# A token-mixing kernel: first pair of each pass on raw operands, 64-row tiles at the pass change, eight operand blocks loaded early

## The chip, the cores and the metric

The kernel runs on one core of one Trainium2 chip. The metric is the device time of one execution in microseconds (us). A profiled execution has a span a little below its own time (2212.3 us for a run of 2214.05 us), and the profile of the kernel before happens to be of a run 3 us under the median. So differences between two profiles and differences between two medians do not agree to the microsecond.

Names of the engines: PE is TensorE, DVE is VectorE, ACT is ScalarE, POOL is GpSimd, SP is SyncE. SBUF is the on-chip memory that holds operands, PSUM the one into which products are written. The granted clock is TensorE's clock as the profile shows it, 1.00 being full. The DMA share is the mean busy share of the core's 16 DMA engines; it goes a little over 1 in these views, so it serves for comparison only. A name such as `L850` is line 850 of the kernel that the profile belongs to. Line numbers shift between kernels.

## The reference

The input `x` is (8, 5696, 128). A long convolution along the sequence comes first, then a mixing block. Cut to what matters:

```python
y = irfft(rfft(x, n=2*S, axis=1) * rfft(h, n=2*S, axis=0), n=2*S, axis=1)[:, :S]  # S = 5696
theta = y @ w_theta                          # 128 x 128
zr, zi = y * cos(theta), y * sin(theta)      # "the phases"
u = y + einsum('ts,bsd->btd', w_tok_r, zr) + einsum('ts,bsd->btd', w_tok_i, zi)   # "the mixing"
out = u + relu(u @ w_ch)                     # "the output steps"
```

The mixing is by far the largest part: two 5696 x 5696 matrices against 8 x 128 columns.

## The kernel before

What matters starts near 480 us with the second half of the phases and ends with the last output.

**The phases** transpose a tile of `y` on TensorE, copy it from PSUM (`y_ap`, VectorE), store the copy, compute cos and sin, and store `z` to device memory (`z_hbm`). While they run, the first operand blocks of the mixing are loaded:

```python
    def load_b(p, j, pool):                       # block j of pass p: two parts, 2 x 512 KB
        t_ = pool.tile([P, 7 * 1024], BF16, tag=f"b{j}", name=f"b{j}")
        for z in range(2):
            eng = nc.scalar if z and (p or j >= NE) else nc.sync      # NE = 4
            eng.dma_start(t_[:, z * 2048:(z + 1) * 2048], z_hbm[z, p, j].rearrange(...))
        ...
    def sum_b(bt):                                # operand sums of one block, 128x1024 each
        nc.vector.tensor_sub(bt[M3], b12, b22)
        nc.vector.tensor_sub(bt[M4], b21, b11)
        nc.vector.tensor_add(bt[M1], b11, b22)
        nc.vector.tensor_add(b12, b11, b12)       # in place: the raw operand is gone
        nc.vector.tensor_add(b21, b21, b22)       # in place
    ...
    for n, ti in enumerate(tile_order):
        phase_step(ti, 1)
        if n in (7, 15, 19):
            load_b(0, next(early), bpe)           # then the fourth after the loop
```

**The mixing** contracts in two passes, p = 0 and 1, over halves of the sequence. A pass has 11 operand blocks (`b0` to `b10`, 1 MB each) that stay in SBUF and are read by everything in the pass. It treats 22 *pairs* of 128-row tiles by a scheme of seven products in place of eight (as Strassen's), on sums of operands (`sum_b`) and sums of weights (`w_sum`): 7 x 22 = 154 products of 128x512 a pair. Weights come in by POOL's DMA queue into six buffers, are transposed by VectorE (`w_t`), and summed by VectorE. In pass 0 the results go to device memory; in pass 1 they are fetched, added and turned into output ("output steps", woven between later products).

The last 64 rows make a *64-row tile* of 88 products in each pass, called `None` in the order:

```python
        pairs = (list(range(11)) + [None] + list(range(11, 22)), list(range(22)) + [None])
        ...
            if tt == 0:                           # before the products of the pass's first pair
                for j in range(nj):
                    sum_b(bts[j0 + s0 + j])
        ...
            for n, q in enumerate(ORDER):         # seven products
                for j in range(nj):
                    for r in range(2):
                        nc.tensor.matmul(ms[q], a[q][:, j, :, r], bts[jj][q][:, r, :], ...)
```

The blocks of pass 1 take the place of those of pass 0, so block j of pass 1 is loaded when the last reader of block j in pass 0 has finished. That stretch, from the end of pair 21 of pass 0 to the second pair of pass 1, is called the *pass change* below. Where a 64-row tile stands elsewhere, its 19.2 or 19.6 us are added to make kernels comparable.

Of the kernel before, what the change touches and what calls it, by code (L numbers as in the profile page):

```python
# [10 lines left out]
F32 = mybir.dt.float32  # L11
BF16 = mybir.dt.bfloat16
F16 = mybir.dt.float16
add = mybir.AluOpType.add
# [8 lines left out]
def kernel(  # L23
# [492 lines left out]
    ORDER = (M3, M4, M5, M2, M1, M7, M6)  # L516

    wp = ctx.enter_context(tc.tile_pool(name="wpool", bufs=6, side="right"))
    NE = 4
    bpe = ctx.enter_context(tc.tile_pool(name="bpool_e", bufs=1, side="right", reuse_waits="tile"))  # L520
    bts_of = {0: [], 1: []}

    def load_b(p, j, pool):

        t_ = pool.tile([P, 7 * 1024], BF16, tag=f"b{j}", name=f"b{j}")
        for z in range(2):
            eng = nc.scalar if z and (p or j >= NE) else nc.sync
            eng.dma_start(t_[:, z * 2048:(z + 1) * 2048],
                          z_hbm[z, p, j].rearrange("i (s r) n -> (i s) (r n)", r=2))
        bt = [t_[:, k * 2048:(k + 1) * 2048].rearrange("p (r q n) -> p r q n", r=2, q=2)[:, :, q, :]  # L530
              for k in range(2) for q in range(2)]
        bt += [t_[:, q * 1024:(q + 1) * 1024].rearrange("p (r n) -> p r n", r=2) for q in range(4, 7)]
        bts_of[p].append(bt)
# [8 lines left out]

    for step in steps0:
        step()
    early = iter(range(NE))
    for n, ti in enumerate(tile_order):
        phase_step(ti, 1)
        if n in (7, 15, 19):
            load_b(0, next(early), bpe)
    for j in early:  # L550
        load_b(0, j, bpe)
    pha.close()
    xa.close()
    psp.close()
# [3 lines left out]
    with tc.tile_pool(name="bpool", bufs=1, reuse_waits="tile") as bp, \  # L558
# [17 lines left out]
                            ap=[[S, 32], [32 * S, ng], [1, nj * 64]]))  # L576
            return wb

        def w_t(wb, j0, nj, ng=4):
            wt = tp.tile([P, TJ, P, 2], BF16, tag="wt")  # L580
            nc.vector.transpose(  # L581
                wt.rearrange("p j t r -> p (j t r)").bitcast(F32).rearrange(
                    "p (j g t) -> p g j t", j=TJ, g=4)[:, :ng, :nj],
                wb[:, :ng, j0 * 64:(j0 + nj) * 64].bitcast(F32).rearrange(
                    "p g (j s) -> p g j s", j=nj))
            return wt
# [125 lines left out]
                zl_of[p] = zl  # L712


        pairs = (list(range(11)) + [None] + list(range(11, 22)), list(range(22)) + [None])
        chunks = [(p, tt, c) for p in range(2) for tt in pairs[p] for c in range(len(CHUNKS))]
        stretches = []
        for k, (p, tt, c) in enumerate(chunks):
# [18 lines left out]
        def prepare(i, at_once=True):  # L737
            if i >= len(stretches):
                return None
            k, p, tt, j0, s0, nj = stretches[i]  # L740
            if s0 == 0:
                loads(k + 1)
            if tt is None:
                a1, a2 = (w_t(wb, s0, nj, ng=2) for wb in loaded[k])
                return a1, a2, w_sum(a1, a2, add, nj, m=64)
            w11, w22, w12, w21 = loaded[k]
            a = {}

            def step(n):

                if n == 0:
                    a[M3] = w_t(w11, s0, nj)
                elif n == 1:
                    a[M4] = w_t(w22, s0, nj)
                elif n == 2:
                    a["12"] = w_t(w12, s0, nj)
                    a[M5] = w_sum(a[M3], a["12"], add, nj)
                elif n == 3:
                    a["21"] = w_t(w21, s0, nj)
                    a[M2] = w_sum(a["21"], a[M4], add, nj)  # L760
                elif n == 4:
                    a[M1] = w_sum(a[M3], a[M4], add, nj)
                elif n == 5:
                    a[M7] = w_sum(a["12"], a[M4], ALU.subtract, nj)
                else:
                    a[M6] = w_sum(a["21"], a[M3], ALU.subtract, nj)
            if at_once:
                for n in range(7):
                    step(n)
                return a  # L770
            return a, step
# [3 lines left out]
        for i, (k, p, tt, j0, s0, nj) in enumerate(stretches):  # L775
            first_of_pair = j0 + s0 == 0
            end_of_pair = j0 + s0 + nj == NJ
            if first_of_pair and tt == 0:
                start_pass(p)
                if p == 0:  # L780
                    spread += [bg_phase(t, h) for t in list(range(22, 34)) + [44] + list(range(34, 44))
                               for h in range(2)]
                    spread += [bg_left(g) for g in range(0, NT, 4)]
                    spread[0][0]()
                    spread[1][0]()
                    nxt = prepare(0)
            bts, zl = bts_of[p], zl_of[p]
            if tt == 0:
                for j in range(nj):
                    sum_b(bts[j0 + s0 + j])  # L790

            woven = (tt is not None and end_of_pair and i + 1 < len(stretches)
                     and stretches[i + 1][2] is not None)
# [3 lines left out]
            if tt is None:  # L797


                if first_of_pair:  # L800
                    ps = [mps.tile([P, 512], F32, tag=f"m{q}", name=f"m{q}") for q in (M3, M4)]
                    cs = [addend(p, h, NT - 1, h, m=64) for h in range(2)]
                a1, a2, sa = a
                for j in range(nj):
                    jj = j0 + s0 + j
                    for r in range(2):
                        b = [x[:, r, :] for x in bts[jj]]
                        st_ = jj == 0 and r == 0
                        sp_ = jj == NJ - 1 and r == 1 and zl is None
                        for h, x0, q0, x1, q1 in ((0, sa, M2, a2, M4), (1, a1, M3, sa, M5)):  # L810
                            nc.tensor.matmul(ps[h][:64], x0[:, j, :64, r], b[q0],  # L811
                                             start=st_, stop=False)
                            nc.tensor.matmul(ps[h][:64], x1[:, j, :64, r], b[q1],  # L813
                                             start=False, stop=sp_)
                if end_of_pair:
# [5 lines left out]
                    for h in range(2):  # L821
                        c, c0 = cs[h]
                        nc.vector.tensor_add(c[:64], c0[:64], ps[h][:64])
                        finish(p, NT - 1, h, c, m=64)
                continue
            if first_of_pair:
                ms = [mps.tile([P, 512], F32, tag=f"m{q}", name=f"m{q}") for q in range(7)]
                where = ((tt, 1), (22 + tt, 0), (tt, 0), (22 + tt, 1))
                if zl is not None:
                    wl = [wlp.tile([P, P], BF16, tag=f"wl{n}", name=f"wl{n}") for n in range(2)]  # L830
                    for n in range(2):
                        nc.sync.dma_start(wl[n], wl_hbm[:, 22 * n + tt, :])
            if j0 + s0 == 2 * TJ:
                cs = [addend(p, n, t, h) for n, (t, h) in enumerate(where)]
            left = {}
            if zl is not None and end_of_pair:
                left = {M5: (wl[0], zl[1]), M7: (wl[0], zl[2]),
                        M2: (wl[1], zl[0]), M6: (wl[1], zl[2])}
            if end_of_pair:
                (c12, z12), (c21, z21), (c11, z11), (c22, z22) = cs  # L840
                sums = {M3: ((c12, z12, add), (c22, z22, add)), M4: ((c11, z11, add), (c21, z21, add)),
                        M5: ((c11, c11, ALU.subtract), (c12, c12, add)),
                        M2: ((c21, c21, add), (c22, c22, ALU.subtract)),
                        M1: ((c11, c11, add), (c22, c22, add)),
                        M7: ((c11, c11, add),), M6: ((c22, c22, add),)}
            for n, q in enumerate(ORDER):
                for j in range(nj):
                    jj = j0 + s0 + j
                    for r in range(2):
                        nc.tensor.matmul(ms[q], a[q][:, j, :, r], bts[jj][q][:, r, :],  # L850
                                         start=(jj == 0 and r == 0),
                                         stop=(jj == NJ - 1 and r == 1 and q not in left))
                if q in left:
                    nc.tensor.matmul(ms[q], left[q][0], left[q][1], start=False, stop=True)  # L854
                if end_of_pair:
                    for c, z, op in sums[q]:
                        nc.vector.tensor_tensor(c, z, ms[q], op=op)  # L857
                    if woven:
                        for n_ in {1: (0, 1), 2: (2,), 3: (3,), 4: (4,), 5: (5,), 6: (6,)}.get(n, ()):
                            step(n_)  # L860


                if n == 1 and spread and (p == 1 or not end_of_pair):
                    where_bg["tags"] = ("c2", "c3") if j0 + s0 == TJ else ("red", "mag")
                    _, first, second = spread.pop(0)
                    first()
                    if len(spread) > 1:
                        spread[1][0]()
                if n == 4 and second is not None:
                    second()  # L870
                    second = None
            if not end_of_pair:
                continue
            finish(p, tt, 1, c12)
            finish(p, 22 + tt, 0, c21)
            finish(p, tt, 0, c11)
# [34 lines left out]
```

## Time and profile before

| | before |
|---|---|
| median of 3 runs | 2216.57 us (2213.73 to 2218.0) |
| profiled span | 2212.3 us |
| first product of the mixing | 549.6 us |
| second pair of pass 0 begins | 611.5 us |
| pass change with both 64-row tiles | 95.8 us |
| last product of the mixing to the end | 18.7 us |

The first view is the page's picture of the span in 40 equal slices (55 us each), each digit the busy tenths of a slice, for the kernel before.

```profile
PE   3788888755799999999999997999999999999997
DVE  7767766747888887868886776977777686877773
PEclk8689899878999999999999998999999999999998
DMA  7357464588989989888999879688787979787872
```

From slice 12 on TensorE is at 9 everywhere except where the pass changes (slice 25, near 1360 us) and at the very end. So there are three places to gain: the step from the phases into the mixing (slices 9 to 11), the pass change, and the tail. The second view is busy time by stretch, before. The columns are: stretch, its length, busy us (and instructions) of PE, weight loads, DVE, ACT and POOL, then TensorE's granted clock, the DMA share and GB/s.

```profile
553.00:576.00 23.00, 18.55 (x81) 7.94 (x79) 19.86 (x37) 3.14 (x5) 6.05 (x12) 0.93 1.02 351
590.00:620.00 30.00, 24.56 (x105) 10.03 (x105) 30.00 (x57) 5.02 (x8) 8.62 (x16) 0.94 0.65 130
650.00:700.00 50.00, 50.00 (x260) 23.77 (x259) 43.43 (x85) 16.12 (x26) 27.70 (x52) 1.00 0.92 166
1331.00:1385.00 54.00, 38.89 (x161) 15.76 (x160) 35.13 (x69) 0.00 (x0) 19.11 (x36) 0.87 1.10 305
```

Read them in turn. In 650 to 700 us, a steady stretch, TensorE is busy 50.00 of 50.00 at clock 1.00. At the start of the mixing the DMA engines are full first (share 1.02, 351 GB/s) and then VectorE is (30.00 of 30.00). At the pass change the DMA engines are full (1.10, 305 GB/s).

The third view is the chain of waits, before (start, us, what): what a product costs in the steady part, and the last output steps.

```profile
628.38 5.18 PE m L850 x24
...
2193.15 0.43 PE m L820 x2
...
2195.17 0.70 DVE c L671
...
2197.67 0.70 DVE c L671
...
2208.02 0.68 DVE c L671
```

24 products in 5.18 us are 0.216 us each, so 154 products are 33.3 us, and 176 are 38.0. The last product is at 2193 us; six output steps in series (2.4 to 2.8 us each) follow.

The Trainium skill gives two figures for this ("TensorE: Matmul & The Clock Gate", section "Back-to-back issue gap"): N/2.4 + 2.5 ns at full clock, which is 216 ns for 512 columns, called the isolated case, and about 131 ns as the sustained figure of a real kernel. This trace shows the former, 216 ns, throughout the steady part.

The fourth view is what TensorE waited for at the pass change (1290 to 1440 us), before: waiter, releaser, us in total, times, longest; and one row of its timeline there (start, us, instruction, idle before it).

```profile
PE m L850 <- DVE out__18393 L590: 9.4, 1, 9.4
```

Note also the six products in 2.74 us, 0.43 us apart: after that idle time the granted clock was 0.50 (1370 to 1380 us). The skill states this rule (same page, "Part 1: The HAM clock gate"): half rate after an idle window of about 3.4 us. The trace agrees as far as an idle time of 9.4 us goes; the limit itself was not measured here.

### The profile page before, as it was taken

The page shows a single profiled execution, that of the slowest core. Times are in us where ns is not written, and L with a number is a line of the kernel's source. Part 1 is how long each engine was busy: PE and PEld are TensorE (multiplying, and loading weights), DVE is VectorE, ACT ScalarE, POOL GpSimd, SP SyncE. Part 2 cuts the span into 40 slices and gives each one's busy share as a digit, 9 for nine tenths or more (in the row PEclk, how much of TensorE's full clock was granted, in tenths as well). Part 3 has the DMA queues.
Part 4 walks back from the last instruction along what each step waited for, and adds up shares of the span by engine and source line. Part 5 has one row for each costly group of instructions (what it writes and reads, how often), then busy time and mean ns, then how long its engine had stood idle before and what let it go on. Part 6 is the DMA issues. An engine that isn't in the chain of part 4 may idle for free.

```text
span 2212.3 us, 41297 instructions
## 1 busy us (share of the span) xinstructions
PE 2015.5 (91%) x15679; PEld 1123.8 (51%) x15679; DVE 1648.3 (75%) x2980; ACT 671.6 (30%) x984; POOL 859.6 (39%) x1568
## 2 busy tenths in 40 slices
PE   3788888755799999999999997999999999999997
PEld 3787888643244444444444442344444444444443
DVE  7767766747888887868886776977777686877773
ACT  5877777556223323223310000011111111111111
POOL 5301010020344545454557543445453545454450
PEclk8689899878999999999999998999999999999998
DMA  7357464588989989888999879688787979787872
GB/s 142 85 131 166 135 141 140 162 195 209 238 165 186 171 174 170 167 147 170 168 180 150 149 135 295 90 147 145 132 153 127 158 128 159 126 153 134 147 132 52
DMA packets 409383, 340.38 MB, mean 154 GB/s; under 512 B 83303, under 2 KB 363751, under 8 KB 408071
## 3 DMA queue, kind: packets, MB, share of 16 engines
q0 software_dynamic: 221312, 143.00, 48.0%
q1 hardware_dynamic: 184992, 185.18, 29.0%
q10 hardware_dynamic: 2880, 9.57, 1.1%
q8 instruction: 123, 2.02, 0.4%
q14 instruction: 76, 0.62, 0.1%
HBM read 381.83 MB, written 97.93 MB: 217 GB/s over the span
## 4 chain that ended last, share of the span: by engine, by line
PE 63%; DVE 3%; DMA 3%; POOL 2%; issue 1%; ACT 0%; DVEq 0%; SPq 0%; ACTq 0%; POOLq 0%
PE m L850 58%; DMA wb<-in_moe_w_tok_r_dram 2%; POOL wb L572 1%; DVE c L857 1%; DMA wb<-in_moe_w_tok_i_dram 1%; PE v L669 1%; PE utp L662 1%; PE m L811 1%; PE m L813 1%; PE m L854 1%; DVE wt L581 1%; PE tpz L611 0%; PE theta_ps L380 0%; POOL wl L630 0%; DMA z_hbm<-mag 0%
## 5 line engine op out<-in xcount | busy, mean ns | idle before, releaser
L572 POOL DMA_DIRECT2D wb<-in_moe_w_tok_i_dram x720 | 390.1, 552 | 776.9 <-DVE wt L581 703.8
L572 POOL DMA_DIRECT2D wb<-in_moe_w_tok_r_dram x720 | 388.5, 553 | 292.0 <-ACT red L401 163.7
L850 PE MATMUL m<-b,wt 128*128 128x512 bf16 x1936 | 454.9, 381 | 6.6 <-DVE wt L581 5.9
L581 DVE STREAM_TRANSPOSE wt<-wb 128x384 f32<-128x384 f32 (+2 forms) x720 | 358.9, 522 | 121.9 <-PE m L850 72.2
L850 PEld LDWEIGHTS <-wt 128*128 128x128 bf16 x1936 | 189.7, 98 | 240.1 <-issue 9.8
L857 DVE TENSOR_TENSOR c<-c,m 128x512 f32<-128x512 f32 x440 | 282.9, 668 | 0.0
L664 ACT ACTIVATE uts<-utp 128x512 bf16<-128x512 bf16 (+1 forms) x90 | 53.3, 592 | 616.4 <-PE utp L662 616.4
L320 PE MATMUL ps<-r_u,u_t 128*128 128x128 f16 x1024 | 137.3, 231 | 16.3 <-DVE u_t L304 10.1
L321 PE MATMUL ps<-r_v,v_t 128*128 128x128 f16 x1024 | 136.1, 231 | 0.0
L659 ACT ACTIVATE ub<-c 128x512 bf16<-128x512 f32 (+1 forms) x90 | 56.5, 628 | 225.4 <-DVE c L857 225.2
L320 PEld LDWEIGHTS <-u_t 128*128 128x128 f16 x1024 | 108.1, 106 | 13.8 <-DVE u_t L304 13.8
L127 POOL DMA_DIRECT2D x<-in_x_dram x64 | 34.2, 540 | 197.2 <-PE ps L190 186.8
L321 PEld LDWEIGHTS <-v_t 128*128 128x128 f16 x1024 | 106.9, 105 | 6.8 <-issue 5.2
L302 ACT ACTIVATE xs<-ps 128x1024 f16<-128x1024 f32 x96 | 95.3, 1019 | 14.7 <-DVE v_t L304 8.4
L304 DVE TENSOR_TENSOR u_t<-xs,hs 128x1024 f16<-128x1024 f16 x96 | 69.8, 727 | 36.8 <-ACT xs L302 21.6
L190 PE MATMUL ps<-f_t,x 89*128 89x180 f16 x512 | 84.8, 311 | 7.7 <-ACT xs L302 5.5
L208 PEld LDWEIGHTS <-w_t 64*128 64x128 f16 x3240 | 63.8, 105 | 41.7 <-issue 27.1
L190 PEld LDWEIGHTS <-x 89*128 89x128 f16 x512 | 73.8, 237 | 9.6 <-issue 9.1
L382 ACT ACTIVATE red<-theta_ps,magic 128x512 f32<-128x512 f32 (+1 forms) x46 | 31.6, 687 | 147.2 <-PE theta_ps L380 93.1
L613 ACT ACTIVATE yb<-tpz 128x512 bf16<-128x512 bf16 (+1 forms) x46 | 27.5, 597 | 160.0 <-PE tpz L611 134.9
L671 DVE SCALAR_TENSOR_TENSOR c<-v,c 128x512 f32<-128x512 f32 (+1 forms) x90 | 61.4, 682 | 11.1 <-PE v L669 10.4
L304 DVE TENSOR_TENSOR v_t<-xs,hs 128x1024 f16<-128x1024 f16 x96 | 67.6, 704 | 0.0
(2846 smaller groups left out, 3789.8 us busy)
## 6 DMA issues: line engine op xcount, KB each, us to landing
wb<-in_moe_w_tok_r_dram POOLq DMA_DIRECT2D x352, 96.0 KB, 4.4
wb<-in_moe_w_tok_i_dram POOLq DMA_DIRECT2D x352, 96.0 KB, 4.8
wb<-in_moe_w_tok_r_dram POOLq DMA_DIRECT2D x352, 80.0 KB, 4.3
wb<-in_moe_w_tok_i_dram POOLq DMA_DIRECT2D x352, 80.0 KB, 3.8
hs<-hf_hbm SPq DMA_DIRECT2D x192, 128.0 KB, 3.3
cp_hbm<-c SPq DMA_DIRECT2D x88, 256.0 KB, 2.1
c<-cp_hbm SPq DMA_DIRECT2D x88, 256.0 KB, 4.4
out_dram<-c SPq DMA_DIRECT2D x88, 256.0 KB, 4.2
```

Of the source, the lines that this page charges most:

```text
L190: nc.tensor.matmul(ps[:, i // 2, (i % 2) * 2 * K1:(i % 2 + 1) * 2 * K1], lhs(q + i), f1_t[:NB], start=True, stop=True)
L208: nc.tensor.matmul(ps[:, e, j * HD:(j + 1) * HD], w_t2[rows, c0 + j, N2 * (1 - ri):N2 * (3 - ri)], a_st["a"][rows, ri * K1 + c0 + j, :], s ...
L302: nc.scalar.activation(xs[:, :, :, :ck], ps, AF.Copy)
L304: nc.vector.tensor_tensor(uv[r][:, :, :, c0:c0 + ck], xs[:, :, :, :ck], hv[:, r:r + 1, :, :ck].to_broadcast([P, 2, HD, ck]), op=mult)
L320: nc.tensor.matmul(o, u_t[:, at:at + P], r_u, start=True, stop=False)
L321: nc.tensor.matmul(o, v_t[:, at:at + P], r_v, start=False, stop=True)
L572: nc.gpsimd.dma_start(wb[32 * i:32 * i + 32, :ng, :nj * 64], bass.AP(tensor=a.tensor, offset=a.offset + row0 * S + p * H + i * QR + j0 * 6 ...
L581: nc.vector.transpose(wt.rearrange("p j t r -> p (j t r)").bitcast(F32).rearrange("p (j g t) -> p g j t", j=TJ, g=4)[:, :ng, :nj], wb[:, : ...
L659: nc.scalar.activation(ub[:m].rearrange("p b d -> p (b d)"), c[:m], AF.Copy)
L671: nc.vector.scalar_tensor_tensor(c[:m], v[:m], 0.0, c[:m], op0=ALU.max, op1=ALU.add)
L850: nc.tensor.matmul(ms[q], a[q][:, j, :, r], bts[jj][q][:, r, :], start=(jj == 0 and r == 0), stop=(jj == NJ - 1 and r == 1 and q not in left))
L857: nc.vector.tensor_tensor(c, z, ms[q], op=op)
```

## The change

The intent: at the start of each pass, do not make the first pair wait for operand sums and weight sums. It uses eight plain products on the raw operands; the sums follow behind its products, for the second pair. One thing that the intent does not name: the first stretch of pass 0 no longer takes up a background unit (a piece of the phases of other rows), so its first pair carries two of them in place of three. The 64-row tiles move to the pass change (last in pass 0, first in pass 1), so that a short tile frees the old blocks and consumes the new ones. Eight blocks in place of four are loaded during the phases, and four `y` buffers in place of two let the stores fall behind. The loads of pass 1 all go to the scalar queue. Cut to its core:

```diff
-    NE = 4
+    NE = 8
@@ load_b
-            eng = nc.scalar if z and (p or j >= NE) else nc.sync
+            eng = nc.scalar if p or j >= NE else nc.sync
@@ second half of the phases
+    sides["phases"]["sby"] = pool("s2y4", 4, pha, reuse_waits="tile")     # was 2
     for n, ti in enumerate(tile_order):
         phase_step(ti, 1)
-        if n in (7, 15, 19):
-            load_b(0, next(early), bpe)
-    for j in early:
-        load_b(0, j, bpe)
+        if n % 4 == 3:
+            while len(bts_of[0]) < min(n // 2, NE):
+                load_b(0, len(bts_of[0]), bpe)
@@ order
-        pairs = (list(range(11)) + [None] + list(range(11, 22)), list(range(22)) + [None])
+        pairs = (list(range(22)) + [None], [None] + list(range(22)))
@@ prepare: weights of a first pair, transposed only
+            if tt == 0:
+                a = [w_t(w11, s0, nj), w_t(w12, s0, nj), w_t(w21, s0, nj, pool=sp), w_t(w22, s0, nj, pool=sp)]
+                return a if at_once else (a, lambda n: None)
@@ 64-row tile: raw operands in pass 1
+                terms = (((a1, M2, a2, M7), (a1, M6, a2, M5)) if sa is None else
+                         ((sa, M2, a2, M4), (a1, M3, sa, M5)))
@@ products
-            if tt == 0:
-                for j in range(nj):
-                    sum_b(bts[j0 + s0 + j])
+            classic = tt == 0
+            if classic:
+                for n in range(4):                      # 4 x 2 x 2 x nj: eight products
+                    for j in range(nj):
+                        for r in range(2):
+                            for h in range(2):
+                                nc.tensor.matmul(ms[n // 2 * 2 + h], a[n][:, j, :, r],
+                                                 bts[jj][n % 2 * 2 + h][:, r, :], ...)
+                    aside(n == 0, n == 2)               # background work; none in the first stretch
+                for j in range(nj):
+                    sum_b(bts[j0 + s0 + j])             # now behind the products
+                ...                                     # 4 additions from PSUM, were 12
```

## The prediction

> **What bounds the kernel now.** From 620 to 2193 us TensorE bounds the mixing: in the table of equal stretches it is busy 50 of 50 us almost everywhere at clock 1.00, and in the chain of waits 24 products of 128x512 take 5.18 us, 0.216 us each. Counting products per stretch at that duration gives TensorE's losses:
>
> 1. First pair of pass 0: its 154 products run from 549.6 to 611.5 us (timeline), 62 us where 33 would do. First it waits for operand loads (351 GB/s, 553 to 576 us), then VectorE is full (590 to 620 us) with operand sums (55, one per 0.60 us) besides weight transposes and sums.
> 2. Pass change (1330 to 1430 us): about 28 us. DMA is at its maximum (305 GB/s, share 1.10, 1331 to 1385 us), then VectorE is full for 30 us.
>
> Smaller: 5 us in 1150 to 1330, and a tail of 19 us after the last product (six output steps, 2.8 us each for full ones).
>
> **What the change does.** It adds 22 products to each first pair: 9.5 us of TensorE in all. It removes 60 VectorE instructions: 40 weight sums, 16 additions from PSUM, 4 sums of the 64-row tile. The 55 operand sums stay, but the first pair no longer needs them; in the instruction order three of five per block are hoisted into the phases or beside the loads, two wait for that block's raw products. Eight blocks instead of about four arrive during the phases.
>
> **Costing.**
> - Phases: five more MB at 0.36 MB/us are 14 us of DMA in a 60 us stretch now at 0.78 of 1.10: nearly full. Stores wait behind loads; four y buffers absorb that. I take the phases to end within 4 us of now.
> - First pair: 176 products (38 us) and two background units (0.9 us), no stall that I find in VectorE's order: 39.5 us instead of 62. Saves about 20 us net.
> - Pass change: two 64-row tiles (19 us each) release, then consume blocks. Blocks need 32 us of DMA, weights before the first pair some 15 us, so the pair starts near 50 us after the first 64-row tile, not 38: 12 us of loss remain of 28. Less 4.75 us of products: saves about 11. The loads move to the scalar queue; the Trainium skill (Trainium Kernel Development and Optimization, Key Constraints) says that all queues run on the same 16 engines and only issue time is saved, so I count no bandwidth for that. The trace agrees so far: both queues together gave 351 GB/s.
> - End: pair 21 is last, four output steps instead of six: saves about 4 us.
>
> Sum: about 35 us, 1.6%.
>
> **Predicted: 2181 us, 2166 to 2198 eight times in ten. Faster by over 2%: 0.20; within 2%: 0.79; slower: 0.01.**
>
> **What would show it.** First pair of pass 0 near 40 us, TensorE full; raw-block sums of VectorE inside the phases; the second 64-row tile stretched to 28 to 32 us, TensorE waiting for operand blocks; first pair of pass 1 near 40 us; tail near 15 us; steady stretches still 0.216 us per product.
>
> **What would make it wrong.** Loads delaying the phases' stores, or hoisted sums waiting for loads at the head of VectorE's queue, lengthening the phases by 10 us; or four buffers removing the phases' present waits (23 us of TensorE waiting for the y copy), bringing it under 2172. At the pass change, weights and blocks may share DMA worse than I count, or better.

## More of the kernel before

Medians are of three to seven executions.

```profile
1373.71 2.74 PE L850 MATMUL m<-b,out__18393 128*128 128x512 bf16 x6 [9.44 <-DVE out__18393 L590]
```

The first pair of pass 1 stands 9.4 us for a weight sum. VectorE's timeline there shows why that sum was late:

```profile
1372.04 0.58 DVE L581 STREAM_TRANSPOSE wt<-wb 128x384 f32<-128x384 f32 x1 [8.56 <-DMA wb<-in_moe_w_tok_i_dram]
...
1373.11 0.54 DVE L590 TENSOR_TENSOR out__18393<-wt 128x768 bf16<-128x768 bf16 x1
```

VectorE stood 8.56 us for the *load* of the weights; the transpose and the sum followed within 2 us. So the longest wait here was for a late load in front of VectorE, and not for the work of summing.

## The result, and the profile after

| | before | after |
|---|---|---|
| median (4 runs each) | 2217.28 us | 2194.34 us (2191.57 to 2197.7) |
| ratio of the means | | 0.9899 (0.9879 to 0.9918) |
| profiled span | 2212.3 us | 2192.6 us |

A ratio here is the mean time of one kernel's fast runs over that of the other's of the same rounds, so not quite the ratio of the medians. The bracket is a 95% interval. The kernel is 1% faster: within the predicted range, inside the 2% band, but about 13 us short of the predicted middle.

Where the 19.6 us between the two profiles (unrounded spans) come from (milestones read from TensorE's timeline):

| stretch | before | after | difference | predicted |
|---|---|---|---|---|
| start to first product of the mixing | 549.6 | 555.6 | +5.9 | within 4 |
| first pair of pass 0 | 61.9 | 40.7 | -21.2 | 39.5 us long |
| rest of pass 0, without its 64-row tile | 730.8 | 727.6 | -3.2 | |
| pass change, both 64-row tiles included | 95.8 | 100.3 | **+4.5** | **-11** |
| rest of pass 1 | 755.4 | 753.8 | -1.6 | |
| tail | 18.7 | 14.7 | -4.0 | -4 |

The first pair of pass 0 in TensorE's timeline, after:

```profile
555.56 14.94 PE L856 MATMUL m<-b,wt 128*128 128x512 bf16 x60 [0.67 <-ACT mag L400]
...
596.26 2.75 PE L886 MATMUL m<-b,wt 128*128 128x512 bf16 x12
...
601.25 1.46 PE L886 MATMUL m<-b,out__10528 128*128 128x512 bf16 x6 [2.01 <-DVE c L869]
```

The raw pair runs from 555.56 to 596.26 us without a pause over 1 us. A new small wait of 2.0 us appears behind it: the second pair's third product needs a PSUM bank that the raw pair's additions (`L869`) still read.

The stretches and the tail of the kernel after, as shown of before:

```profile
550.00:590.00 40.00, 36.31 (x173) 16.79 (x173) 31.63 (x59) 7.30 (x12) 17.22 (x32) 0.88 1.08 251
650.00:700.00 50.00, 50.00 (x257) 23.61 (x255) 40.66 (x81) 17.73 (x29) 25.78 (x48) 1.00 1.00 182
1330.00:1370.00 40.00, 31.46 (x134) 15.05 (x132) 16.96 (x33) 0.00 (x0) 12.47 (x23) 0.91 1.11 338
1370.00:1380.00 10.00, 2.04 (x5) 0.90 (x6) 6.06 (x12) 0.00 (x0) 4.26 (x8) 0.58 0.77 161
```

```profile
2177.24 0.14 DVE c L893
...
2188.59 0.69 DVE c L670
```

The tail is four output steps now, behind pair 21's additions. The pass change is the place that disagrees with the prediction. In 1370 to 1380 us TensorE does 2.04 us of work in 10, *while the DMA share falls to 0.77*: something other than bandwidth holds it. TensorE's waits in 1290 to 1440 us, after:

```profile
PE m L814 <- DVE wt L580: 9.5, 2, 8.7
PE m L812 <- DVE c L824: 7.0, 1, 7.0
```

Both releasers are on VectorE, and VectorE is far from full (16.96 busy of 40 in 1330 to 1370 us). VectorE's timeline, after, shows what stood at the head of its queue:

```profile
1348.72 0.69 DVE L537 TENSOR_TENSOR b<-b 128x1024 bf16<-128x1024 bf16 x1 [1.80 <-DMA b<-z_hbm]
1349.32 1.27 DVE L824 TENSOR_TENSOR c<-yy,m 64x512 f32<-64x512 bf16 x2
...
1362.49 0.43 DVE L710 TENSOR_TENSOR zl<-zl,zl 128x512 bf16<-128x512 bf16 x1 [8.08 <-DMA zl<-zl_hbm]
1362.83 0.68 DVE L537 TENSOR_TENSOR b<-b 128x1024 bf16<-128x1024 bf16 x1
1363.43 0.56 DVE L580 STREAM_TRANSPOSE wt<-wb 128x192 f32<-128x192 f32 x2
...
1373.94 1.96 DVE L580 STREAM_TRANSPOSE wt<-wb 128x384 f32<-128x384 f32 x4 [8.78 <-DMA wb<-in_moe_w_tok_r_dram]
...
1377.60 0.76 DVE L580 STREAM_TRANSPOSE wt<-wb 128x128 f32<-128x128 f32 x2
```

Read it from the top. The first 64-row tile's products were done at 1343, but its two additions (`L824`), which free the PSUM banks that the second tile writes, ran only at 1349.32, behind sums of blocks 3 and 4 that waited 1.75 and 1.80 us for their loads. Then a small sum of the last rows' operands (`L710`) waited 8.08 us for a load, and held a transpose that would have freed a weight buffer. The four transposes of the *next pair* then waited 8.78 us for weights at the head of the queue, and the last transposes that the second 64-row tile needs (1377.60) stood behind them. TensorE went on at 1377.95 us.

That an instruction waits behind another whose data has not come is what the Trainium skill says of the queue ("TensorE: Matmul & The Clock Gate", the table at the top, row "Engine queue depth"): VectorE's queue is strictly first in, first out, 8 deep. The trace agrees with the order, with 7.0 and 8.7 us of TensorE's time beside it; no run here shows the depth.

### The profile page after: what moved, and what is told of

Its sections match the earlier page's. It is cut to its first block, busy times and chain, and to the rows that moved or that the text cites. A ratio compares the mean times of both kernels' runs of the same rounds, so it can differ in the third digit from the quotient of the medians.

```text
span 2192.6 us, 41307 instructions
## 1 busy us (share of the span) xinstructions
PE 2018.6 (92%) x15723; PEld 1132.8 (52%) x15723; DVE 1619.2 (74%) x2920; ACT 669.1 (31%) x984; POOL 859.3 (39%) x1568
## 4 chain that ended last, share of the span: by engine, by line
PE 78%; DMA 7%; DVE 6%; ACT 4%; issue 2%; POOL 1%; SPq 1%; DVEq 0%; ACTq 0%; POOLq 0%
PE m L886 60%; PE m L856 4%; PE ps L320 3%; PE ps L321 3%; PE ps L190 2%; DMA hs<-hf_hbm 2%; DMA wb<-in_moe_w_tok_r_dram 2%; DVE c L893 1%; ACT xs L302 1%; PE ps L343 1%; PE ps L208 1%; DMA y_hbm<-y_ap 1%; PE utp L661 1%; PE v L668 1%; DVE u_t L304 1%
## 5 line engine op out<-in xcount | busy, mean ns | idle before, releaser
L886 PE MATMUL m<-b,wt 128*128 128x512 bf16 x1848 | 426.8, 379 | 2.4 <-DVE wt L580 2.4
L886 PEld LDWEIGHTS <-wt 128*128 128x128 bf16 x1848 | 180.8, 98 | 220.8 <-DVE wt L580 3.3
L893 DVE TENSOR_TENSOR c<-c,m 128x512 f32<-128x512 f32 x420 | 270.2, 668 | 0.4 <-PE m L886 0.4
L320 PE MATMUL ps<-r_u,u_t 128*128 128x128 f16 x1024 | 136.9, 231 | 16.2 <-DVE u_t L304 10.9
L856 PE MATMUL m<-b,wt 128*128 128x512 bf16 x352 | 79.5, 385 | 0.7 <-ACT mag L400 0.7
```

Source lines behind the costliest of these rows:

```text
L320: nc.tensor.matmul(o, u_t[:, at:at + P], r_u, start=True, stop=False)
L856: nc.tensor.matmul(ms[n // 2 * 2 + h], a[n][:, j, :, r], bts[jj][n % 2 * 2 + h][:, r, :], start=(n % 2 == 0 and jj == 0 and r == 0), stop= ...
L893: nc.vector.tensor_tensor(c, z, ms[q], op=op)
```

## The experiments

Theory A: at the pass change the change loses time because a late load at the head of VectorE's queue holds unrelated work; elsewhere it does what the prediction said. The rivals were, by experiment: the loads themselves (bandwidth) set the pass change; the early loads lengthen the phases; the gain of the first pair comes from the early loads or the buffers, not from the eight products. Twelve kernels ran in three batches, each batch on one chip beside seven runs of the kernel before (medians 2217.01, 2217.84, 2217.15 us). All gave correct results.

| run | what | median us | ratio to before (95%) |
|---|---|---|---|
| after | the change | 2194.34 | 0.9899 (0.9879 to 0.9918) |
| e1 | after, four early loads | 2201.35 | 0.9931 (0.9916 to 0.9947) |
| e2 | after, pass 1's 64-row tile in mid-pass | 2234.93 | 1.0085 (1.0066 to 1.0103) |
| e3 | after, VectorE's order fixed | 2189.18 | 0.9879 (0.9853 to 0.9904) |
| e4 | after, other PSUM banks for the second tile | 2192.38 | 0.9894 (0.9878 to 0.9911) |
| e5 | before, early loads and four buffers | 2205.53 | 0.9958 (0.9936 to 0.9979) |
| e6 | after, seven products in pass 1's first pair | 2184.48 | 0.9856 (0.9838 to 0.9873) |
| e7 | before, four buffers | 2206.06 | 0.9956 (0.9939 to 0.9972) |
| e8 | e2, output steps taken up in the tile | 2185.04 | 0.9864 (0.9842 to 0.9887) |
| e9 | e8, VectorE's order fixed | 2191.11 | 0.9882 (0.9861 to 0.9902) |
| e10 | e6, VectorE's order fixed | 2181.14 | 0.9834 (0.9815 to 0.9854) |
| e11 | after, two buffers | 2202.58 | 0.9935 (0.9914 to 0.9956) |
| e12 | after, both 64-row tiles where they were | 2188.45 | 0.9868 (0.9850 to 0.9887) |

### e1: four blocks loaded early, as before

```diff
-    NE = 8
+    NE = 4
-        if n % 4 == 3:
-            while len(bts_of[0]) < min(n // 2, NE):
-                load_b(0, len(bts_of[0]), bpe)
+        if n in (7, 15, 19):
+            load_b(0, len(bts_of[0]), bpe)
+    load_b(0, 3, bpe)
```

> The changed kernel with operand blocks loaded as before the change (three in the phases, one at their end, the other seven on both queues after them); four y buffers stay. Theory A (the early loads lengthen the phases by about 6 us but free the DMA engines for the weights of the third and fourth stretch): the first product comes near 550 us instead of 555.6, the third stretch then waits for weights, and the total is within 5 us of 2194 on either side. Rival B (the early loads are pure gain): phases no shorter, total 2205 or more. Rival C (they are pure cost): total 2188 or less.

The phases ended at 543.0 us, earlier than before. The raw pair then took 59.9 us, nearly as long as the seven-product pair of before (61.9), and the second pair began at 602.9 us against 596.3 in the kernel after. The largest wait of this stretch that the kernel after does not have and the wait for operand blocks, in TensorE's waits (475 to 610 us), and ScalarE's timeline ahead of it (ACTq is its queue, issuing DMA):

```profile
PE theta_ps L380 <- ACT yb L612: 9.5, 2, 8.8
PE m L856 <- DMA b<-z_hbm: 0.8, 2, 0.4
```

```profile
548.81 14.80 ACTq L528 DMA_DIRECT2D b<-z_hbm  x7
563.66 0.69 ACT L382 ACTIVATE red<-theta_ps,magic 128x512 f32<-128x512 f32 x1 [16.02 <-DMA b<-z_hbm]
```

ScalarE also issues loads of the blocks from the fifth on in this kernel: seven of them took its queue 14.80 us, and the next activation (`red`, which reads no operand block) stood for 16.02 us. The copy `yb` that TensorE waited for is later in the same queue. The kernel before has waits of the same kind there (9.5 us in all). So the eight products alone did not shorten the first pair. But TensorE waited only 0.8 us for blocks themselves. It stood behind ScalarE's background work, which stood behind the *issue* of the loads: seven loads took ScalarE's queue 14.80 us here, six took it 3.29 us in the kernel after. The raw products ended at 595.8 us, and from 590 to 603 VectorE was full (13.00 of 13) with the sums put off and the next transposes. Whether late blocks, or only their issue on ScalarE's queue, make the pair long was not separated; four early blocks with the rest loaded by SyncE would do it. The total was 7 us above the kernel after (medians), outside theory A's margin of 5 and below rival B's range.

### e2: the 64-row tile of pass 1 in the middle of the pass

```diff
-        pairs = (list(range(22)) + [None], [None] + list(range(22)))
+        pairs = (list(range(22)) + [None], list(range(11)) + [None] + list(range(11, 22)))
```

> Second pass: the 64-row tile moved from its start to its middle (on sums again), so that the pair on raw operands follows the first 64-row tile at once. Theory A (at the pass change the second 64-row tile eats a block in 1.7 us while DMA brings one in 2.9 us, and VectorE's queue stands still behind sums that wait for loads): the pair on raw operands takes 3.5 us a block and hides the loads; total 2175 to 2182. Rival B (the loss at the pass change is DMA time that must be paid wherever the tile stands): 2190 to 2194.

A miss, and slower than before. The pass change itself was better: the raw pair began at 1347.3 us, directly behind the first tile, and the second pair at 1392.2 (1424.2 after). But behind the tile in the middle of pass 1 the last 11 pairs took 436.5 us, where the first ten pairs behind the raw one took 366.9. TensorE's waits in 1800 to 2210 us, e2:

```profile
PE utp L661 <- DVE c L670: 19.4, 10, 2.2
```

Nearly all of the waits are for output steps and additions (`utp`, `v`, `c`). My reading was that two output steps stay pending after the tile, because no step is taken up during its products, and the six buffers for addends are then all held until late. That was argued, so e8 tests it.

### e3: VectorE's order fixed at the pass change

The transposes of the second tile and of the first pair are pinned in program order, the first tile's additions stand ahead of the operand sums, and the sum of the last rows' operands (`zl`) comes late.

```diff
+            if pin["on"]:
+                pin["last"] = tc.keep_in_program_order(ins)          # in w_t
+                        if p == 0:
+                            tc.keep_in_program_order(ins)            # the tile's additions
-                for j in range(nj):
-                    sum_b(bts[j0 + s0 + j])
+                with (tc.issue_after(pin["sums"].ins) if p else ExitStack()):
+                    for j in range(nj):
+                        sum_b(bts[j0 + s0 + j])
-                nc.vector.tensor_add(zl[2], zl[0], zl[1])            # moved to the pair's end
```

> Same work and same place of the 64-row tile, but VectorE's order at the pass change is fixed: weight transposes of that tile and of the next pair, and the first tile's additions, go ahead of the operand sums; the sum of the last rows' operands goes to the end of the pair. Theory A (10 us of the loss are VectorE standing at the head of its queue for a load that nobody urgently needs): the waits of 7.0 and 8.7 us shrink, the pair on raw operands starts about 10 us earlier (near 50 us after the first 64-row tile instead of 60), total 2182 to 2188. Rival B (pure DMA): start unchanged, total 2192 to 2196.

The two tiles took 52.1 us instead of 59.8, and the pass change 93.4 instead of 100.3. TensorE's waits in 1300 to 1440 us, e3, and the two stretches behind the tiles:

```profile
PE m L820 <- DMA b<-z_hbm: 8.2, 6, 2.1
PE m L818 <- DMA b<-z_hbm: 1.9, 2, 1.2
```

```profile
1384.00:1404.00 20.00, 19.79 (x99) 8.95 (x99) 20.00 (x37) 0.38 (x1) 7.10 (x14) 1.00 0.66 97
1404.00:1424.00 20.00, 18.16 (x86) 8.22 (x86) 20.00 (x36) 1.57 (x3) 5.79 (x11) 1.00 0.50 74
```

The two waits for VectorE are gone, and what is left are waits for the operand blocks themselves: 52 us is what the loads allow, near the 50 that the prediction had worked out. Behind the tiles VectorE is now full, 20.00 of 20.00 twice, with the sums that were put off. Theory A holds for the pass change. The total is 1 us outside theory A's range; its interval overlaps with that of the kernel after, so it is the trace, not the total, that carries the verdict.

### e4: only the PSUM banks of the second tile

```diff
-for q in (M3, M4)]
+for q in ((M1, M5) if p else (M3, M4))]
```

> Only the second 64-row tile gets two other PSUM banks than the first, so it need not wait for the first tile's additions. Theory A (VectorE's later stand for weights, 8.7 us, sets the end of the tile anyway): the 7.0 us wait is gone but the later wait grows by about as much, total 2192 to 2196. Rival B (the shared banks cost their 7 us by themselves): total 2186 to 2189.

TensorE's waits in 1290 to 1440 us, e4:

```profile
PE m L814 <- DVE wt L580: 14.3, 3, 6.5
```

The 7.0 us wait for the first tile's additions has gone, and the wait for transposed weights has grown from 9.5 to 14.3 us. The tiles took 60.0 us, as before this edit. One wait was a cover over the other.

### e5: the kernel before with eight early loads and four buffers

```diff
-    NE = 4
+    NE = 8
+    sides["phases"]["sby"] = pool("s2y4", 4, pha, reuse_waits="tile")
 ... the loading loop of after
```

> The kernel before with the early loading alone: eight blocks in the phases, four y buffers; seven products in both first pairs, 64-row tiles in their old places. Theory A (most of the gain at the first pair is that the first pair no longer waits for VectorE's operand sums): first product near 556 us, first pair 45 to 52 us, second pair from about 605 us against 611.5 before and 596.3 in the changed kernel; total 2207 to 2214. Rival B (the gain is the early loading, the eight products add nothing): second pair from 597 us or sooner, total 2202 or less.

The first product came at 557.65 us and the second pair at 600.1, so the *seven*-product pair took 42.5 us. The eight products of the kernel after take 40.7. The result lies between the two theories: loading early shortens the first pair nearly as much with seven products. The loads do not act by bandwidth alone: in this pair VectorE is busy 37.1 us, against 52.7 in the first pair of e7 (which loads as before), because sums of the early blocks are made during the phases: the first of the five sums has been made for seven blocks when the mixing starts, for two in e7. But the phases are 8 us longer than before, so the second pair begins only 11 us earlier, and the total (2205.53 us) is no better than that of e7 below, which has the four buffers and none of the early loads.

### e6: seven products in the first pair of pass 1

```diff
-            classic = tt == 0
+            classic = tt == 0 and p == 0
+            if tt == 0 and p == 1:
+                for j in range(nj):
+                    sum_b(bts[j0 + s0 + j])
```

> The changed kernel with eight products in the first pass only; the first pair of the second pass takes seven products on sums again, still after the second 64-row tile. Theory A (at the pass change DMA and VectorE's stands at the head of its queue bound, and three of the five sums of a block are ready beside the loads anyway, so seven products would do): the pair is 4 to 5 us shorter, total 2189 to 2194. Rival B (VectorE's sums bound this pair as in the kernel before): pair 45 us or longer, total 2198 or more.

Better than both theories said: 10 us below the kernel after, with intervals that do not overlap. The tiles took 52.8 us, the pair 36.7, the pass change 89.6 us (100.3 after). The wait for the first tile's additions is still there, the wait for transposes is nearly gone, and loads show up (TensorE's waits, 1300 to 1440 us):

```profile
PE m L815 <- DVE c L827: 6.9, 1, 6.9
PE m L817 <- DMA b<-z_hbm: 3.3, 2, 2.0
PE m L817 <- DVE wt L580: 1.3, 1, 1.3
```

So in pass 1 the eight products cost time. My reading of the traces: the 64-row tile now in front of the pair meets the loads first, and when it ends all blocks have been there for some time and their sums are done or under way. The raw pair has no wait left to avoid. In neither kernel does TensorE wait for a load in this pair. It pays 22 more products, 4.75 us, and in the kernel after its transposes also stand ahead of the tile's in VectorE's queue.

### e7: the kernel before with four `y` buffers and nothing else

```diff
+    sides["phases"]["sby"] = pool("s2y4", 4, pha, reuse_waits="tile")
```

> The kernel before with four y buffers in the second half of the phases and nothing else. Theory A (two buffers make the phases wait for their stores; four save about 6 us of phases, as the run with the old loading showed with its first product at 543 us): first product near 543 us; the first pair then waits longer for the remaining blocks, so of 6 us some 2 to 4 arrive: total 2212 to 2215. Rival B (all 6 arrive): 2210 to 2211. Rival C (the buffers do nothing by themselves): first product near 550 us, total 2216 to 2218.

No theory of mine expected this much: 2206.06 us, 11.8 below the kernel before of the same batch. That is half of what the whole change gains. The first product came at 541.75 us (549.6 before), the second pair at 603.6 (611.5). VectorE's waits in the phases (475 to 556 us), first before, then e7, then e11 (see below):

```profile
DVE y_ap L480 <- DMA y_hbm<-y_ap: 13.5, 4, 9.0
```

```profile
DVE y_ap L480 <- DMA y_hbm<-y_ap: 5.0, 3, 2.2
```

```profile
DVE y_ap L480 <- DMA y_hbm<-y_ap: 11.9, 4, 9.8
```

With two buffers VectorE stood up to 9.0 us for a store to leave the buffer that it was to fill, and TensorE waited for VectorE. TensorE's wait for that copy, from 475 us to the first product, is 23.2 us before and 16.2 in e7, 30.2 in e11 and 21.1 in the kernel after. The prediction had seen the 23 us and named the buffers as what might remove them, but it put nothing for them into its sum.

### e8: e2, with output steps taken up during the tile

```diff
                 a1, a2, sa = a
+                drained = None
+                if p == 1 and spread:
+                    _, first, drained = spread.pop(0)
+                    first()
 ... the tile's products ...
+                if drained is not None:
+                    drained()
```

> As the run with the second 64-row tile in the middle of the second pass, but output steps are taken up during that tile too, one in each of its four stretches. Theory A (that run lost 59 us after the tile because two more output steps stayed pending to the end and the six buffers of addends ran out, while the pass change itself gained 13 us or more): no loss after the tile, total 2172 to 2182. Rival B (the tile in the middle of the second pass costs something else): total 2200 or more.

The loss behind the tile vanished: the last 11 pairs took 394.5 us (436.5 in e2). The stretch 2000 to 2050 us, first in e2, then in e8:

```profile
2000.00:2050.00 50.00, 47.64 (x248) 22.54 (x252) 33.24 (x66) 5.69 (x10) 23.57 (x44) 1.00 0.80 133
```

```profile
2000.00:2050.00 50.00, 49.74 (x260) 23.98 (x265) 35.00 (x69) 5.80 (x10) 27.59 (x52) 1.00 0.91 156
```

This shows that the pending output steps were the cause in e2 (that the six buffers are the way it acts is still only argued). The total, 2185.04 us, is 3 us above theory A's range.

### e9: e8 with VectorE's order fixed and other PSUM banks

```diff
+            pin["on"] = p == 1 and tt == 0 and j0 + s0 <= TJ        # pins as in e3
-for q in range(4 if classic else 7)]
+for q in ((M2, M1, M7, M6) if classic else range(7))]
```

> As the run with the second 64-row tile in the middle and its output steps taken up, and with VectorE's order fixed at the pass change (transposes for the first two stretches of the pair on raw operands and the first tile's additions ahead of the operand sums, the sum of the last rows' operands at the pair's end), and the pairs on raw operands in the four PSUM banks that the next pair uses last. Theory A (what is left of the loss there, 4.9 and 3.7 us of waits, is again VectorE standing at the head of its queue): total 2174 to 2180. Rival B (it is DMA): 2183 to 2187, unchanged. Rival C (the sums, pushed back, now come too late for the second pair): 2188 or more.

Worse than e8, 2191.11 us, as rival C said. TensorE's waits in 1290 to 1440 us and one stretch, e9:

```profile
PE m L868 <- DVE wt L582: 7.8, 3, 4.5
PE m L903 <- DVE wt L582: 4.5, 1, 4.5
```

```profile
1390.00:1400.00 10.00, 5.54 (x21) 2.06 (x20) 10.00 (x18) 0.00 (x0) 1.85 (x4) 0.88 0.55 74
```

VectorE is full here (10.00 of 10) while TensorE works 5.54. My reading: without a second tile at the pass change there is less time in which the sums can be made, and holding them back moves them into the stretch where the next pair's transposes are due. The order of e3 helped where VectorE was waiting, and hurt where it was busy. As the banks were changed in the same run, the order's share is argued, not tested alone.

### e10: e6 with VectorE's order fixed

```diff
             if tt == 0 and p == 1:
-                for j in range(nj):
-                    sum_b(bts[j0 + s0 + j])
+                with tc.issue_after(added.ins):            # the first tile's additions
+                    for j in range(nj):
+                        sum_b(bts[j0 + s0 + j])
+                if j0 + s0 == 2 * TJ:                      # zl sum: late
+                    tc.keep_in_program_order(nc.vector.tensor_add(zl[2], zl[0], zl[1]))
```

> As the run with seven products in the first pair of the second pass, and with the operand sums of that pass held behind the first 64-row tile's additions, the sum of the last rows' operands late in the pair, and the first pass's raw pair in the banks that the next pair uses last. Theory A (the 6.9 us wait of TensorE for those additions is a sum waiting for a load ahead of them; after it the blocks' loads bound the second tile): the wait goes, the tile still ends with its last block, total 2178 to 2184. Rival B (nothing but DMA bounds it): 2183 to 2187. Rival C: sums held back make the pair longer, 2188 or more.

Not in the cut: the raw pair of pass 0 also uses the banks of e9. That can be worth little here, since in e6 the wait for its additions was only 0.2 us (2.0 after).

TensorE's waits in 1290 to 1460 us, e10:

```profile
PE m L819 <- DMA b<-z_hbm: 8.6, 6, 2.1
PE m L817 <- DMA b<-z_hbm: 2.1, 2, 1.5
```

The 6.9 us wait for VectorE has gone, and waits for loads of 10.7 us have taken its place: the tiles take 52.85 us, where e6 had 52.8. Beneath the wait lay the loads. The pass change is 89.2 us. At 2181.14 us this is the fastest kernel run here and it beats both the kernel before and the kernel after, but its interval overlaps with that of e6, so I do not claim that the fixed order adds to e6.

### e11: the kernel after with two `y` buffers

```diff
-    sides["phases"]["sby"] = pool("s2y4", 4, pha, reuse_waits="tile")
```

> The changed kernel with the two y buffers of before. Theory A (four y buffers by themselves are worth about 10 us, as the run of the kernel before with four showed, and more here, where more loads stand between the stores): phases 8 to 14 us longer, total 2202 to 2210. Rival B (with eight early loads the phases are bound by DMA and not by the y buffers): total 2193 to 2198.

The first product came at 567.5 us (555.6 after), the second pair at 606.9 (596.3), the total was 8 us more. The waits are the third fence under e7. With e7 this shows the worth of the buffers with and without the rest: 8 to 12 us.

### e12: the kernel after with both 64-row tiles in their old places

```diff
-        pairs = (list(range(22)) + [None], [None] + list(range(22)))
+        pairs = (list(range(11)) + [None] + list(range(11, 22)), list(range(22)) + [None])
```

> The changed kernel with both 64-row tiles in their places of before (middle of the first pass, end of the second), the first pairs still on raw operands. Theory A (the pair on raw operands alone, 3.5 us a block, hides the loads; moving both tiles to the pass change brings two consumers of 1.7 us a block there and costs more than it gives): pass change better by 8 to 12 us than in the changed kernel, tail longer by 4: total 2184 to 2190. Rival B (the move is what makes room for the loads): total 2198 or more.

2188.45 us, 6 below the kernel after (the intervals overlap slightly, but every run of e12 is below every run of the kernel after). The second pair of pass 1 begins 47.9 us after the end of pair 21, so the pass change is 47.9 + 38.8 (two tiles elsewhere) = 86.7 us against 100.3. Some is given back: the rest of pass 0 is 4.1 us longer and the tail 3.9 us. 13.6 - 4.1 - 3.9 = 5.6 us, which accounts for the total. There is still one wait at the change (TensorE's waits, 1290 to 1460 us, e12):

```profile
PE m L856 <- DVE c L893: 7.3, 1, 7.3
```

VectorE's timeline shows theory A's mechanism once more: six of pair 21's additions (`L893`), for which TensorE waited, ran only from 1352.05, behind a transpose that stood 4.23 us for its weights.

The raw pair, 38.9 us of products, runs here while the blocks arrive, and only 9 us are lost. In the kernels with seven products there and no tile in between, the same stretch took 57.0 us (before) and about 56 (e5) and 57 (e7), against 47.9. So the raw pair does gain 8 to 9 us where it directly follows pair 21; the loads' queue differs as well and was not tested apart. In the kernel after a 64-row tile of 19 us runs while the blocks arrive, and the pair comes when they are there. That the longer work hides the loads better is the likely reason; part of the 13.6 us is the order of VectorE's queue, since e3 gains 7 by that alone.

## Why the prediction was right or wrong

**Total.** 2181 us was predicted with a range of 2166 to 2198; 2194.34 was measured. Right in its range and in its class, with about 13 us less gain than the middle said. The parts do not all agree, and two errors of opposite sign partly cancel.

**First pair of pass 0: right in size, half wrong in its cause.** "39.5 us instead of 62" was 40.7. But the prediction counted the eight products and the early blocks as one step and did not ask which does the work. e1 shows that with four early blocks the eight products take 59.9 us, and e5 that with eight early blocks the seven products take 42.5. Loading early shortened the pair; whether by the blocks being there, by their sums made in the phases or by ScalarE's queue being free (see e1) stays open. Of the moment that counts, the start of the second pair (611.5 before, 596.3 after), the four buffers alone account for 7.9 us (e7); early loads and eight products together for the other 7.3. Early loads without the eight products gave 3.5 of these (e5), the eight products without the early loads 0.7 (e1). That suggests that the two work together, but these are single profiles, and both figures are within the spread given next.

**Phases: a missing term.** "I take the phases to end within 4 us of now" was +5.9 us in the profiled execution. Kernels with the same code up to there had their first product between 550.4 and 559.6 us, so this figure is good to some 4 us. Underneath are two larger terms: the buffers took 8 us off (e7) and the early loads put 13 to 16 us on (e7 to e5: 541.75 to 557.65; e1 to after: 543.0 to 555.6). The prediction named the buffers only among the things that could make it wrong and gave them no microseconds. They are worth a third (e11) to half (e7) of the total gain.

**Pass change: the step that failed.** The prediction said "12 us of loss remain of 28. Less 4.75 us of products: saves about 11." Measured was a loss of 22.6 us (100.3 less 38.8 for the tiles and 38.9 for the pair's 180 products) where before it had been 22.9 (95.8 less 38.8 and 34.1 for 158 products): hardly any loss was removed, and the 22 more products came on top, so +4.5 us. About 5 us of the error are in the starting figure, 28 for 22.9. Nearly 11 us are in the loss that remains, 22.6 for 12. The wait that was wrong is the one in the second 64-row tile: the prediction had it "stretched to 28 to 32 us, TensorE waiting for operand blocks". It took 40.6 us, and TensorE waited there for VectorE (16.5 us) and not once for a block. The DMA part of the sum was nearly right: "the pair starts near 50 us after the first 64-row tile" is what e3 and e10 show, 52.3 and 52.8 us, when VectorE's order is fixed (e3's second tile takes 32.9 us and does wait for blocks; e6, with the order as it was but without the raw pair's transposes, has its pair start at 52.9). The kernel after needed 59.8. The missing 7 to 8 us are VectorE's queue: additions, and transposes that the tile needs, stood behind instructions whose loads had not landed. The prediction says "no stall that I find in VectorE's order" of the first pair of pass 0 only, and nothing of that order at the pass change. The other 3 us are 1.3 in the tiles even in e3's order (52.1 less 38.8, for 12) and 1.6 in the raw pair, 40.5 us for 38.9 of products, with two output steps of the first tile woven in.

VectorE stood like this before the change as well, 8.56 us for a weight load. The intent aims at the sums; products that need no sums still need those weights.

A second thing there was not asked at all: whether both halves of the change are wanted at the same place. e6 shows that the eight products in pass 1 cost 10 us once a 64-row tile stands before them, and e12 that without the move of the tiles the pair on raw operands gains 8 to 9 us there and the whole is 6 us faster.

**Queues.** "I count no bandwidth" for the scalar queue is not contradicted: with the loads of pass 1 all on it, the pass change ran at a share of 1.11 (338 GB/s in 1330 to 1370 us), against 1.10 and 305 before, in stretches that differ in what else was loaded. That is what the skill's page "Trainium Kernel Development and Optimization" (section "Key Constraints") says. e1 adds the other side: where ScalarE issued loads, its own work stood for 16.0 us, and TensorE behind it for 8.8.

**Tail: right.** "Four output steps instead of six: saves about 4 us" was 18.7 to 14.7, -4.0 us.

**What stays open.** Why e6's second tile no longer waits for transposes was read from the order of instructions, not tested by itself. The spread of the phases (550 to 560 us with equal code) has no cause here. A version with the tiles in their old places and seven products in pass 1, or with e12's first wait removed, was not run; it may beat e10. Nor was the scalar queue for the loads of pass 1 tested by itself.

## What to carry to other kernels

When a wait is to be removed by cheaper first work, follow it back first: the sum that TensorE waited for at the pass change was itself waiting for a load. Then ask which instruction meets the late data after *all* parts of the change, because a part that moves other work in front of it can make the cheap start pointless. On an engine that takes its queue in order, list every instruction that waits for a load, and what stands behind it, at each place where loads are late, and do not stop at the first place checked. Before adding early loads to a stretch, look at what its copies wait for: here a second pair of store buffers, one line, gave a third to half of the whole gain.

## What the Trainium skill lacked or had wrong

- "TensorE: Matmul & The Clock Gate", section "Back-to-back issue gap", gives about 131 ns as the sustained spacing of 512-column products in a real kernel, and calls 216 ns the isolated case. The runs show 216 ns sustained (24 products in 5.18 us), with weight loads between them.
- "TensorE: Matmul & The Clock Gate", the table at the top, has VectorE's queue as strictly in order and 8 deep. The row does not say what the order can cost: late loads ahead of VectorE's work held TensorE for 7.0 us and for 8.7 us at one pass change, the second time with the DMA share down to 0.77.
- "Trainium Kernel Development and Optimization", section "Key Constraints", says that issuing from several queues saves issue time. It lacks the reverse: where ScalarE issued operand loads between its activations (e1), an activation stood for 16.0 us, and TensorE behind ScalarE's copy for 8.8 us.
- The skill advises double buffers and names the buffer count as a possible cause of idle time, but no page that I used has a way to count store buffers: here two `y` buffers made VectorE wait 13.5 us for stores in the phases, four 5.0, and that was worth 8 to 12 us of 2217.
